# Moving attention transposes of two batches from TensorE to crossbar DMA, with the attention units on fixed slots

## The chip, the cores and the metric

One core of one Trainium2 chip. The metric is the device time of one execution in microseconds. Of every kernel there is one profiled execution and several timed ones, taken in turn with the kernel before on the same chip.

## The reference, cut to what matters

Four batches, 8 heads, 768 positions, head dimension 64. Each query attends to the keys within 16 positions and to 24 block summaries: the maximum of each block of 32 keys, with the mean of the block's values. The result, as 3072 tokens of 512 features, goes through a gated feed-forward layer.

```python
k_sum = k.reshape(B, H, nb, block, D).max(axis=3)
v_sum = v.reshape(B, H, nb, block, D).mean(axis=3)
scores_l = scale * np.matmul(q, k.transpose(0, 1, 3, 2))       # masked to |i - j| < 16
scores_s = scale * np.einsum('bhsd,bhnd->bhsn', q, k_sum) + np.log(block)
a = softmax(concatenate([scores_l, scores_s]))
x = (a @ concatenate([v, v_sum]))                              # 3072 x 512
out = (1 / (1 + np.exp(-(x @ w_gate))) * (x @ w_val)) @ w_out  # 512 -> 1536 -> 512
```

## The kernel before

The core works in four stages. Stage b runs the feed-forward of batch b on TensorE, and between its units ("m1": eight matmuls of 384 columns, "m2": six of 512) it places small units of the attention of batch b + 1. A stage has 24 m1 units and 12 m2 units, numbered 0 to 35 here as slots. The attention units:

```python
def T(self, p, h=None):            # a pair of heads: q and k to "dimension on partitions"
    ...                            # 12 TensorE transposes into PSUM (6 for k, 6 for q)
    self.natural(kTn[:, 16:16 + S], pk)                        # ScalarE copies PSUM -> SBUF
    self.natural(self.qT[p][:, 0:S if h is None else HALF], pq)
    nc.vector.tensor_reduce(out=kTx[:, 0, W:KX], ..., op=ALU.max)   # block maxima
    ...                            # two VectorE copies that spread keys and maxima
def S(self, p, hf): ...            # scores, exp on ScalarE, product with the mask on VectorE
def R(self, g, h): ...             # block sums of v, a quarter of four heads, VectorE
def M(self, g, h=None):            # means of four heads to bf16, four small DMAs to row group 96
    nc.vector.tensor_scalar_mul(out=mb, in0=self.ms[g], scalar1=1.0 / 32.0)
    for i in range(4):
        nc.sync.dma_start(out=self.vx[96:120, 0, 4 * g + i, 0:64], in_=mb[NS * i:NS * (i + 1)])
def B(self, *_): self.replicate(1) # ONE DMA, 272 KB: spreads the means over all 12 query tiles
def A(self, p, h=None): ...        # probabilities x [values; means]; needs what B wrote
def X(self, p, h=None): ...        # 6 TensorE transposes of the output, ScalarE copy to xT
# ... (cut)
MEANS = "R0a R0b R0c R0d M0 R1a R1b R1c R1d M1 - B".split()
NEXT = "- - T0 T1 S0a S0b T2 S1a S1b T3 S2a S2b S3a S3b - - A0 A1 X0 A2 X1 A3 X2 X3".split()
    both = [x for pair in zip(MEANS, NEXT) for x in pair]
    extra = (att[b + 1].units(" ".join(both)) + [lambda: loads(b + 2)]
             + att[b + 1].units(" ".join(NEXT[len(MEANS):])))
    spread(m1[0] + m1[1] + ffn.units2(), extra, 0, 33)
```

`spread` deals the 37 entries evenly over 33 slots. That puts M1 at about slot 16, B at slot 20 and the first A at slot 26 (entry number times 33/37).

The softmax here doesn't subtract the row's maximum and nothing guards it: scores larger than these inputs give would overflow.

## Time and profile before

| | before |
|---|---|
| median of 4 runs (range) | 262.46 us (262.02 to 262.8) |
| span of the profiled run | 259.5 us |
| until stage 1 starts / stage 1 / stage 2 / stage 3 | 95.2 / 57.2 / 56.5 / 46.8 us |
| TensorE idle in stage 1 / stage 2 | 0.8 / 0.0 us |

The prediction below shows the lines. How to read them: a row of a table by stretches gives the bounds in the span, the length, then per engine the busy time and the count of instructions. A row of a timeline gives start, length, engine, source line, operation, output<-inputs, shapes and count, and in brackets the idle time of the engine ahead of it and what ended that. A row of the list of waits gives who waited for what: total us, times, longest us. The row "PEclk" of a page is the clock that TensorE was granted, in tenths of full speed. TensorE's rows overlap at their ends, so a cost is read from one start to the next.

### The profile page before, as it was taken

What the parts mean: (1) busy time and instruction counts of PE and PEld (TensorE: products, weight loads), DVE (VectorE), ACT (ScalarE), POOL (GpSimd) and SP (SyncE); (2) the same over time, 40 slices, a digit from 0 to 9 for tenths busy, and PEclk for the clock granted to TensorE, in tenths of its full rate; (3) what the DMA queues carried; (4) which work ended last, traced back from release to release, by engine and by line L of the source; (5) the groups of instructions that cost most, each with busy time, mean ns of one, the idle gap of its engine ahead of it and who ended that gap; (6) DMA issues with size and microseconds to landing.
All of it is one profiled execution on the core that took longest, in us unless ns stands there. A gap on an engine that the chain in (4) does not pass through costs nothing.

```text
span 259.5 us, 5305 instructions
## 1 busy us (share of the span) xinstructions
PE 241.0 (93%) x2136; PEld 137.7 (53%) x2136; DVE 133.8 (52%) x263; ACT 124.5 (48%) x217; POOL 77.1 (30%) x111
## 2 busy tenths in 40 slices
PE   1567899999999998999999999999999999999993
PEld 1432455666644555666555556666555556666441
DVE  5865237648733318888645227988543124444000
ACT  2850347538942434766742435766533433333111
POOL 8998059377000279400002893000000000000000
PEclk9999999999999999999999999999999999999999
DMA  6999999999308999900199999000211220000132
GB/s 223 230 165 170 222 269 278 269 121 123 18 16 230 314 401 134 101 4 1 26 234 317 360 132 133 1 3 1 46 40 51 75 82 0 0 3 1 40 121 81
DMA packets 60912, 32.70 MB, mean 126 GB/s; under 512 B 40624, under 2 KB 57432, under 8 KB 60504
## 3 DMA queue, kind: packets, MB, share of 16 engines
q0 software_dynamic: 45632, 9.31, 41.4%
q1 hardware_dynamic: 14168, 22.28, 27.3%
q10 hardware_dynamic: 1088, 0.79, 0.9%
q8 instruction: 16, 0.26, 0.4%
q14 instruction: 8, 0.07, 0.1%
HBM read 34.34 MB, written 6.29 MB: 157 GB/s over the span
## 4 chain that ended last, share of the span: by engine, by line
PE 82%; DMA 9%; ACT 3%; DVE 2%; issue 1%; SPq 0%; ACTq 0%
PE gp L350 25%; PE vp L350 24%; PE m L367 19%; PE tp L178 4%; DMA qkst<-in_k_dram 3%; DMA out_dram<-ot 3%; PE sc L223 3%; PE vsp L240 3%; DMA qkst<-in_q_dram 3%; PE av L300 2%; PE br L321 2%; ACT kTn L184 1%; DVE kTx L199 1%; DVE vx L120 1%; ACT ot L372 1%
## 5 line engine op out<-in xcount | busy, mean ns | idle before, releaser
L358 DVE SCALAR_TENSOR_TENSOR hT<-gate,vp 128x384 bf16<-128x384 f32 x96 | 52.4, 548 | 56.1 <-PE vp L350 45.2
L350 PE MATMUL gp<-xT,wg 128*128 128x384 bf16 x384 | 80.2, 330 | 1.1 <-ACT xT L324 1.1
L350 PE MATMUL vp<-xT,wv 128*128 128x384 bf16 x384 | 79.6, 329 | 0.8 <-ACT ot L372 0.8
L367 PE MATMUL m<-wo,hT 128*128 128x512 bf16 x288 | 67.1, 380 | 0.0
L357 ACT ACTIVATE gate<-gp 128x384 f32<-128x384 f32 x96 | 47.4, 495 | 40.8 <-DVE hT L358 29.2
L350 PEld LDWEIGHTS <-wv 128*128 128x128 bf16 x384 | 37.8, 98 | 27.3 <-issue 3.0
L350 PEld LDWEIGHTS <-wg 128*128 128x128 bf16 x384 | 35.5, 99 | 21.7 <-issue 0.5
L122 POOL CAST qkbf<-qkst 128x768 bf16<-128x768 f32 (+1 forms) x28 | 22.5, 813 | 78.3 <-DMA qkst<-in_k_dram 38.6
L367 PEld LDWEIGHTS <-hT 128*128 128x128 bf16 x288 | 26.3, 98 | 28.4 <-issue 0.4
L372 ACT ACTIVATE ot<-m 128x512 f32<-128x512 f32 x24 | 14.3, 597 | 47.4 <-PE m L367 44.8
L147 POOL DMA_DIRECT2D vx<-in_v_dram x48 | 36.5, 774 | 0.6 <-DMA vx<-in_v_dram 0.4
L229 ACT ACTIVATE P<-sc 128x768 bf16<-128x768 f32 x32 | 26.0, 815 | 10.9 <-PE sc L223 10.8
L230 DVE TENSOR_TENSOR P<-P,mask 128x768 bf16<-128x768 bf16 x32 | 18.7, 585 | 13.3 <-ACT P L229 13.1
L178 PE MATMUL tp<-ident,qkbf 128*128 128x128 bf16 x192 | 15.5, 236 | 7.7 <-DVE qkbf L120 5.9
L199 DVE TENSOR_REDUCE kTx<-kTn 128x24 bf16<-128x768 bf16 x16 | 15.2, 951 | 7.8 <-ACT kTn L184 7.8
L178 PEld LDWEIGHTS <-qkbf 128*128 128x128 bf16 x192 | 13.4, 106 | 9.8 <-DVE qkbf L120 7.0
L324 ACT COPY xT<-br 128x768 bf16<-128x768 bf16 (+1 forms) x20 | 13.3, 669 | 10.9 <-PE br L321 10.9
L184 ACT COPY kTn<-tp 128x768 bf16<-128x768 bf16 x16 | 12.8, 799 | 9.3 <-PE tp L178 8.7
L268 DVE TENSOR_REDUCE ms<-vm 96x16 f32<-96x512 f32 x16 | 16.4, 1023 | 0.0
L309 DVE TENSOR_TENSOR xs<-av,rec 128x768 bf16<-128x768 f32 (+1 forms) x20 | 15.9, 797 | 0.7
L307 DVE RECIPROCAL rec<-av 128x12 f32<-128x12 f32 (+1 forms) x20 | 4.3, 216 | 22.3 <-PE av L300 22.3
L223 PE MATMUL sc<-qT,kTx 64*128 64x64 bf16 x384 | 12.1, 197 | 3.1 <-DVE kTx L203 2.9
(46 smaller groups left out, 112.0 us busy)
## 6 DMA issues: line engine op xcount, KB each, us to landing
qkst<-in_k_dram SPq DMA_DIRECT2D x16, 384.0 KB
out_dram<-ot SPq DMA_DIRECT2D x24, 256.0 KB
qkst<-in_q_dram SPq DMA_DIRECT2D x12, 384.0 KB
vx<-in_v_dram POOLq DMA_DIRECT2D x40, 96.0 KB, 4.7
vm<-in_v_dram SPq DMA_DIRECT2D x4, 768.0 KB
wo<-in_moe_w_out_dram POOLq DMA_DIRECT2D x6, 256.0 KB, 13.6
wg<-in_moe_w_gate_dram POOLq DMA_DIRECT2D x5, 256.0 KB, 8.0
wv<-in_moe_w_val_dram POOLq DMA_DIRECT2D x5, 256.0 KB, 9.8
```

The source lines that it names most:

```text
L122: nc.gpsimd.tensor_copy(out=out, in_=in_)
L147: nc.gpsimd.dma_start(out=vx_t[b % 2][r0:r0 + hi - lo, t, :, 0:64], in_=v[b, :, lo:hi, :].transpose([1, 0, 2]))
L178: nc.tensor.transpose(dst[:, 128 * t:128 * (t + 1)], src[:, t].rearrange("p h d -> p (h d)"), ident)
L199: nc.vector.tensor_reduce(out=kTx[:, 0, W:KX], in_=kTn[:, 16:16 + S].rearrange("p (n w) -> p n w", w=32), axis=AX.X, op=ALU.max)
L223: nc.tensor.matmul(out=sc[:, i, QT * t6:QT * (t6 + 1)], lhsT=kTx[64 * i:64 * i + 64, t, :], rhs=qT[64 * i:64 * i + 64, QT * t:QT * (t + 1) ...
L229: nc.scalar.activation(out=Ph, in_=sc[:, :, 0:6 * QT], func=ACT.Exp, scale=SCALE)
L230: nc.vector.tensor_tensor(out=Ph, in0=Ph, in1=mask[:, None, 6 * hf:6 * hf + 6, :].rearrange("p i t w -> p i (t w)") .to_broadcast([128, 2, ...
L350: nc.tensor.matmul(out=o, lhsT=wb[:, c, 128 * f:128 * (f + 1)], rhs=self.xT[:, c, HALF * hf:HALF * (hf + 1)], start=(c == 0), stop=(c == N ...
L357: nc.scalar.activation(out=gate, in_=gp, func=ACT.Tanh, scale=0.5)
L358: nc.vector.scalar_tensor_tensor(out=self.hT[hf][:, f, :], in0=gate, scalar=1.0, in1=vp, op0=ALU.add, op1=ALU.mult)
L367: nc.tensor.matmul(out=self.m3, lhsT=self.hT[hf][:, f, 128 * tt:128 * (tt + 1)], rhs=wo_bf[:, f], start=(f == 0), stop=(f == NF - 1))
L372: nc.scalar.mul(out=ot, in_=self.m3, mul=0.5)
```

## The change

The intent: TensorE is full, so 144 of its 288 transposes are given to DMA. q and k of batches 2 and 3 are loaded by casting DMAs of GpSimd in their natural layout ("nat") and transposed by DMAs of SyncE (D); the DMA writes what ScalarE copied before; the block maxima become a unit of their own (K). The attention output of these batches goes to xT by DMA (Y). The units are no longer dealt evenly but stand on slots.

```diff
+    def load_nat(tap, b):
+        nat = small()
+        for h in range(H):
+            nc.gpsimd.dma_start(out=nat[:, h // 2, :, 64 * (h % 2):64 * (h % 2) + 64],
+                                in_=tap[b, h].rearrange("(c p) d -> p c d", p=128))
+        return nat
...
+        def D(self, p, h=None):
+            self.begin(p)
+            for dst, nat in ((self.kTn[p][:, 16:16 + S], self.src[0]), (self.qT[p], self.src[1])):
+                nc.sync.dma_start_transpose(out=dst.rearrange("p (c t) -> p c t", c=6),
+                                            in_=nat[:, p].rearrange("p c d -> p (c d)"))
...
+        def Y(self, p, h=None):
+            c0, c1 = (0, 6) if h is None else (3 * h, 3 * h + 3)
+            nc.sync.dma_start_transpose(out=self.xT[:, p, ...], in_=self.xs[p][:, 0:c1 - c0]...)
...
-    MEANS = "R0a R0b R0c R0d M0 R1a R1b R1c R1d M1 - B".split()
-    NEXT = "- - T0 T1 S0a S0b T2 S1a S1b T3 S2a S2b S3a S3b - - A0 A1 X0 A2 X1 A3 X2 X3".split()
+    LATER = """
+        0 D0   1 D1 R0a   2 R0b   3 K0   4 R0c   5 D2   6 S0a R0d   7 K1 M0   8 S0b
+        9 D3 R1a   10 S1a   11 K2 R1b   12 S1b   13 R1c   14 S2a   15 K3 R1d   16 S2b M1
+        18 S3a B   20 S3b   22 A0   23 Y0   25 A1   26 Y1   27 A2   28 Y2   29 A3   30 Y3"""
+    def means(b):               # the two 768 KB loads of v for the block sums
+        if b < B:
+            att[b].L(0)
+            att[b].L(1)
...
+                at[0].append(lambda: loads(b + 2))
...
+                at[17].append(lambda: means(b + 2))
```

The buffers are rearranged too (staging in tiles of "nat" and "vm", four output tiles in place of two).

More of the change, by code (lines that the diff above doesn't have):

```diff
@@ L43 @@
     const = ctx.enter_context(tc.tile_pool(name="const", bufs=1))
-    stg_pool = ctx.enter_context(tc.tile_pool(name="stg", bufs=8))
     bf_pool = ctx.enter_context(tc.tile_pool(name="bf", bufs=10))
+    nat_pool = ctx.enter_context(tc.tile_pool(name="nat", bufs=4))
     vm_pool = ctx.enter_context(tc.tile_pool(name="vmp", bufs=2))
@@ L48 @@
     p_pool = ctx.enter_context(tc.tile_pool(name="pp", bufs=4))
-    xs_pool = ctx.enter_context(tc.tile_pool(name="xsp", bufs=2))
+    xs_pool = ctx.enter_context(tc.tile_pool(name="xsp", bufs=4))
     xT_pool = ctx.enter_context(tc.tile_pool(name="xTp", bufs=2))
@@ L122, in copy, with big, small, load_qk @@
             nc.gpsimd.tensor_copy(out=out, in_=in_)
-    def load_qk(tap, b, p, half=None, queue=None):
+    def big():
+        return vm_pool.tile([128, 2048], FP32, name="vm", tag="vm")
+    def small():
+        return nat_pool.tile([128, NP, 6, 128], BF16, name="nat", tag="nat")
+    def load_qk(tap, b, p, st, half=None, queue=None):
         n = S if half is None else HALF
@@ L128, in load_qk, with staging @@
         T = n // 128
-        st = stg_pool.tile([128, 2, 6, 64], FP32, name="qkst", tag="stg")
         (queue or nc.sync).dma_start(
-            out=st[:, :, 0:T, :].rearrange("p h t d -> p h (t d)"),
+            out=st.rearrange("p h t d -> p h (t d)"),
             in_=tap[b, 2 * p:2 * p + 2, s0:s0 + n, :].rearrange("h (p t) d -> p h (t d)", t=T),
         )
-        return st[:, :, 0:T, :]
+        return st
+    def staging(T):
+        raw = small().rearrange("p a c d -> p (a c d)").bitcast(FP32)
+        return [view(raw, 128 * T * i, [[64 * T, 2], [64, T], [1, 64]]) for i in range(12 // T)]
     def cast_qk(st, eng):
@@ L140, in cast_qk @@
         return bf
+    def load_nat(tap, b):
+        nat = small()
+        for h in range(H):
+            nc.gpsimd.dma_start(
+                out=nat[:, h // 2, :, 64 * (h % 2):64 * (h % 2) + 64],
+                in_=tap[b, h].rearrange("(c p) d -> p c d", p=128))
+        return nat
     def load_v(b, t0, t1):
@@ L172, in __init__ @@
             self.vx = vx_t[b % 2]
-            self.kTx, self.qT, self.P, self.xs = {}, {}, {}, {}
+            self.kTn, self.kTx, self.qT, self.P, self.xs = {}, {}, {}, {}, {}
             self.vm, self.ms = {}, {}
@@ L185, in natural, with begin @@
                            in_=src[:, 0:128 * T].rearrange("p (t a) -> p a t", t=T))
+        def begin(self, p):
+            self.kTn[p], self.kTx[p] = kTn_t[kT_ctr[0] % 2], kTx_t[kT_ctr[0] % 4]
+            kT_ctr[0] += 1
+            self.qT[p] = qT_pool.tile([128, S], BF16, name="qT", tag="qT")
+        def D(self, p, h=None):
+            self.begin(p)
+            for dst, nat in ((self.kTn[p][:, 16:16 + S], self.src[0]), (self.qT[p], self.src[1])):
+                nc.sync.dma_start_transpose(
+                    out=dst.rearrange("p (c t) -> p c t", c=6),
+                    in_=nat[:, p].rearrange("p c d -> p (c d)"))
         def T(self, p, h=None):
+            self.begin(p)
             at = psum2.tile([128, 2, 1024], BF16, name="tp", tag="at")
@@ L192, in T, with K @@
             self.transposed(pq, self.src[p][1])
-            kTn, kTx = kTn_t[kT_ctr[0] % 2], kTx_t[kT_ctr[0] % 4]
-            kT_ctr[0] += 1
-            self.kTx[p] = kTx
-            self.qT[p] = qT_pool.tile([128, S], BF16, name="qT", tag="qT")
-            self.natural(kTn[:, 16:16 + S], pk)
+            self.natural(self.kTn[p][:, 16:16 + S], pk)
             self.natural(self.qT[p][:, 0:S if h is None else HALF], pq)
+            self.K(p)
+        def K(self, p, h=None):
+            kTn, kTx = self.kTn[p], self.kTx[p]
             nc.vector.tensor_reduce(
@@ L260, in L @@
         def L(self, g, h=None):
-            st = self.vm[g] = vm_pool.tile([4 * NS, 32, 64], FP32, name="vm", tag="vm")
+            st = self.vm[g] = big()[0:4 * NS].rearrange("p (w d) -> p w d", d=64)
             nc.sync.dma_start(
@@ L314, in A @@
             self.xs[p] = xs
+        def Y(self, p, h=None):
+            c0, c1 = (0, 6) if h is None else (3 * h, 3 * h + 3)
+            nc.sync.dma_start_transpose(
+                out=self.xT[:, p, 128 * c0:128 * c1].rearrange("p (c t) -> p c t", c=c1 - c0),
+                in_=self.xs[p][:, 0:c1 - c0].rearrange("p c i d -> p (c i d)"))
         def X(self, p, h=None):
@@ L400 @@
     a0 = att[0]
-    sk = [load_qk(k, 0, p) for p in range(NP)]
-    sq = [load_qk(q, 0, p, half=0, queue=nc.scalar) for p in range(NP)]
+    raw = [big(), big()]
+    sk = [load_qk(k, 0, p, view(raw[p // 2], 768 * (p % 2), [[384, 2], [64, 6], [1, 64]]))
+          for p in range(NP)]
+    sq = [load_qk(q, 0, p, st, half=0, queue=nc.scalar) for p, st in enumerate(staging(3))]
     def cast0(p):
@@ L434 @@
     f0.m1(0, 0, 3, 4)
-    def load_next(b):
-        for p in range(NP):
-            s_ = (load_qk(k, b, p), load_qk(q, b, p))
-            srcs[b][p] = [cast_qk(s_[0], "pool"), cast_qk(s_[1], "pool")]
-    for p in range(NP):
-        srcs[0][p].append(cast_qk(load_qk(q, 0, p, half=1), "pool"))
+    for p, st in enumerate(staging(3)):
+        srcs[0][p].append(cast_qk(load_qk(q, 0, p, st, half=1), "pool"))
     for i in range(6):
         load_wo(i)
-    load_next(1)
+    for p in range(NP):
+        st = staging(6)
+        s_ = (load_qk(k, 1, p, st[0]), load_qk(q, 1, p, st[1]))
+        srcs[1][p] = [cast_qk(s_[0], "pool"), cast_qk(s_[1], "pool")]
     load_v(1, 0, NQ)
@@ L451 @@
     LAST = "- - A0 A1 X0 A2 X1 A3 X2 X3"
-    MEANS = "R0a R0b R0c R0d M0 R1a R1b R1c R1d M1 - B".split()
-    NEXT = "- - T0 T1 S0a S0b T2 S1a S1b T3 S2a S2b S3a S3b - - A0 A1 X0 A2 X1 A3 X2 X3".split()
-    def loads(b):
+    LATER = """
[3 more added lines that the diff above has]
+    def means(b):
         if b < B:
@@ L458, in loads @@
             att[b].L(1)
-            load_next(b)
+    def loads(b):
+        if b < B:
+            srcs[b][0], srcs[b][1] = load_nat(k, b), load_nat(q, b)
             load_v(b, 0, NQ)
@@ L466 @@
             spread(m1[0][1:], a0.units(REST), 2, 10)
-            extra = att[1].units(FIRST) + [lambda: loads(2)] + att[1].units(LAST)
+            extra = (att[1].units(FIRST) + [lambda: loads(2), lambda: means(2)]
+                     + att[1].units(LAST))
             spread(m1[1] + ffn.units2(), extra, 4, 23)
         else:
-            extra = []
+            base = m1[0] + m1[1] + ffn.units2()
+            at = {i: [] for i in range(len(base))}
             if b + 1 < B:
-                both = [x for pair in zip(MEANS, NEXT) for x in pair]
-                extra = (att[b + 1].units(" ".join(both)) + [lambda: loads(b + 2)]
-                         + att[b + 1].units(" ".join(NEXT[len(MEANS):])))
-            spread(m1[0] + m1[1] + ffn.units2(), extra, 0, 33)
+                at[0].append(lambda: loads(b + 2))
+                for w in LATER.split():
+                    if w.isdigit():
+                        slot = int(w)
+                    else:
+                        at[slot] += att[b + 1].units(w)
+                at[17].append(lambda: means(b + 2))
+            for i, u in enumerate(base):
+                u()
+                for x in at[i]:
+                    x()
 _INS = ['q', 'k', 'v', 'moe_w_gate', 'moe_w_val', 'moe_w_out']
```

## The prediction

> **What bounds the kernel now.** I read the page's busy line and the 40 slices first, to see whether one engine is full and from when.
>
> ```profile
> PE 241.0 (93%) x2136; PEld 137.7 (53%) x2136; DVE 133.8 (52%) x263; ACT 124.5 (48%) x217; POOL 77.1 (30%) x111
> ...
> PE   1567899999999998999999999999999999999993
> ...
> DMA  6999999999308999900199999000211220000132
> ...
> PE 82%; DMA 9%; ACT 3%; DVE 2%; issue 1%; SPq 0%; ACTq 0%
> ```
>
> TensorE is busy 93% of the span, and nearly all that is missing lies in the first slices, where inputs arrive. The chain that ended last is 82% TensorE too. "Busy" alone would not prove a bound, since matmuls are pipelined, so I next cut the span where the TensorE timeline starts the feed-forward of a new batch (31.91 to 32.11, 95.16, 152.40 and 208.85 us) and asked for the table by stretches. Its columns after the bounds are the length, then the busy time and count of TensorE, its weight loads, VectorE, ScalarE and GpSimd, then granted clock, DMA share, GB/s.
>
> ```profile
> 0.00:32.11 32.11, 18.66 (x165) 10.86 (x166) 18.55 (x51) 13.47 (x25) 23.54 (x42) 1.00 1.48 202
> 32.11:95.16 63.05, 62.69 (x654) 35.99 (x651) 33.28 (x64) 35.48 (x62) 26.71 (x36) 1.00 0.99 197
> 95.16:152.40 57.24, 56.46 (x530) 32.54 (x529) 34.30 (x62) 29.68 (x50) 21.52 (x28) 1.00 0.79 153
> 152.40:208.85 56.45, 56.45 (x530) 32.65 (x529) 34.41 (x62) 29.90 (x50) 5.30 (x8) 1.00 0.39 56
> 208.85:255.60 46.75, 46.75 (x265) 25.63 (x262) 13.30 (x24) 15.34 (x30) 0.00 (x0) 1.00 0.09 34
> ```
>
> The last stretch is pure feed-forward: 24 first-layer units and 12 second-layer half units, 36 units in 46.75 us, so 1.30 us each, at full clock and without a gap. The two before it hold the same feed-forward plus the attention of batch 2 and of batch 3; they are longer by 57.24 - 46.75 = 10.5 us and 56.45 - 46.75 = 9.7 us. TensorE has no idle time in them except one wait of 0.8 us. So each microsecond of TensorE work taken out of them comes off the end time, as long as nothing else comes to stop TensorE. VectorE (34 of 57 us), ScalarE (30) and the DMA engines have room.
>
> What one unit of attention costs is read from the timeline of TensorE as start to next start, not from the mean durations (236 ns per transpose there is a latency, and overlaps its neighbours):
>
> ```profile
> 158.25 0.81 PE L350 MATMUL vp<-xT,wv 128*128 128x384 bf16 x4
> 158.90 0.83 PE L178 MATMUL tp<-ident,qkbf 128*128 128x128 bf16 x12
> 159.57 0.81 PE L350 MATMUL gp<-xT,wg 128*128 128x384 bf16 x4
> ```
>
> ```profile
> 91.90 0.50 PE L321 MATMUL br<-ident,xs 128*128 128x128 bf16 x6
> 92.23 1.46 PE L367 MATMUL m<-wo,hT 128*128 128x512 bf16 x6
> ```
>
> Twelve transposes of one head pair (q and k) move the next matmul by 159.57 - 158.90 = 0.67 us, 56 ns each. The six that turn the attention output cost 92.23 - 91.90 = 0.33 us.
>
> **What the Trainium skill says.** (1) "TensorE: Matmul & The Clock Gate", Part 1, gives 55 to 56 ns from one warm 128-column matmul to the next; this trace agrees (56 ns). Its Part 4 gives about 275 ns for a transpose in a kernel's context; the trace shows a similar duration (236 ns) but not as a cost in the stream, and the stream is what counts here. (2) "VectorE: DVE Perf Modes", The three transpose paths, gives 1309 ns for a 128x128 bf16 block by crossbar DMA. (3) "DMA: Bandwidth & Descriptors", Latency and other measured facts, gives 261 GB/s as an effective rate of transposing DMA, and its section on the anatomy of a DMA about 2 us of fixed cost. (4) The same page, Issuing engines are not separate DMA queues: transfers of all issuers share the 16 DMA engines. The kernel before has no transposing DMA, so it neither confirms nor denies (2) and (3).
>
> **The change part by part.**
>
> Removed from TensorE: for batches 2 and 3, two times 4 head pairs with 12 + 6 transposes. That is 8 x 0.67 + 8 x 0.33 = 5.4 + 2.6 = 8.0 us. The PSUM space that they used is free as well. All of it lies in the two full stretches, thus on the path: **-8.0 us**.
>
> Removed from ScalarE: for each pair two copies of 0.80 us and one of 0.80 us, 8 x 2.4 = 19 us; from GpSimd sixteen casts of 0.86 us, 14 us. Both lie beside TensorE: no direct gain.
>
> Removed from the queue of SyncE: sixteen loads of 384 KB ahead of the output stores. At the start of batch 1 the stores of batch 0 stood behind such loads, ScalarE waited for an output buffer, and TensorE for ScalarE:
>
> ```profile
> 97.40 0.60 ACT L372 ACTIVATE ot<-m 128x512 f32<-128x512 f32 x1 [2.54 <-DMA out_dram<-ot]
> 98.05 0.81 PE L350 MATMUL vp<-xT,wv 128*128 128x384 bf16 x4 [0.78 <-ACT ot L372]
> ```
>
> Without those loads in that queue (only two loads of v, 768 KB each, stay) this wait should go: **-0.8 us**.
>
> Added to GpSimd's queue: 16 casting loads per batch. Twelve loads of v of the same kind (96 x 8 runs of 64 elements; the new ones have 128 x 6, also 768 runs) ran from about 55 to 66 us in the trace:
>
> ```profile
> 54.00:56.00 2.00, 1.00 0.33 51
> 56.00:58.00 2.00, 1.00 1.49 95
> ...
> 64.00:66.00 2.00, 1.00 1.77 108
> 66.00:68.00 2.00, 1.00 0.12 7
> ```
>
> So one takes about 0.95 us, and 16 take 15 us. The instruction order of the changed kernel has them right behind v of batch 1 with no wait for TensorE: k and q of batch 2 should land from 66 to 81 us, v of batch 2 until 93, k and q of batch 3 until 108, v of batch 3 until 120. Batch 2 is needed from 95 us on, so it is in time. It is hidden, but the traffic for batch 3 lies beside the first transposes by DMA.
>
> Added to SyncE's queue: 24 transposes of 128x768 bf16 (196,608 bytes). By (3), an estimate: 0.75 us of transfer + 2 us fixed = 2.8 us each. How much is allowed? The first pair's k is issued after the last store of batch 0, about 0.8 us into stage 1 (as store and next batch overlap before). Its consumer, the block maximum on VectorE, stands behind the fourth unit's gate product, 4 x 1.3 + 0.5 = 5.7 us into the stage: 5 us are allowed. After that VectorE is blocked and TensorE stops about two units later, as PSUM holds two open units; but the 1.7 us of VectorE work behind the wait (0.95 + 0.47 + 0.26) uses most of this. q is needed by the scores behind the seventh unit, 9.1 us into the stage: 8.3 us for two. The outputs' last transpose stands behind unit 30 of 36: 6 x 1.3 - 1.5 (division and store ahead of it) = 6.3 us until the next batch needs it. With 2.8 us each all of this fits. Beside the loads of batch 3 the rate may halve, which makes 3.6 us; still inside. I allow **+0.7 us** on average for stalls at the first pair of a stage and where new slots meet an engine's order.
>
> Moved: the attention units go to fixed slots, with the mask and sum work at the same rate; no count changes, 0 us. Start-up: buffers are shared otherwise, but each cast still waits for one load only, so 0 us.
>
> Sum: 262.6 - 8.0 - 0.8 + 0.7 = 254.5 us, 3.1% less.
>
> **The rivals.** First, **a slow transpose takes over**. If the six blocks of a transfer each cost the 1.3 us of (2), one transfer takes 7.9 us, the 12 of a stage 94 us against about 52 us of TensorE, and the kernel gets some 80 us slower. For it: nothing in the trace measures the operation. Against: 1.3 us for a lone block is mostly fixed cost if (3) holds, and the slots (two transfers per four units, 5.2 us) look placed for about 2.5 us each. Second, **a new wait in VectorE**: transposes of 5 to 7 us beside the loads of batch 3 stop VectorE at the first maximum, TensorE follows, and 1 to 3 us are lost in each stage: 256 to 260 us. For it: DMA share over 1.7 while such loads run. Against: only stage 1 has these loads. Third, **the transposes were hidden anyway**, in gaps of TensorE: time stays at 262. Against: TensorE shows no gaps in stages 1 and 2. Fourth, more is saved than counted: stage 1 is 10.5 us over pure feed-forward, of which 4 pairs at 1.0 us and the 0.8 us wait are known to go; if small restarts go too, 252 us.
>
> **Range and chances.** The saving of 8.0 us is counted and on the path, so the question is only what comes in its place. I take 251.5 to 258.5 as the range: all saved plus a little, or some 4 us lost again. 2% faster is below 257.3, which needs stalls under about 3.5 us in total: 0.78. Within 2%: 0.14. Slower by over 2% needs transposes near 6 us or more throughout: 0.08.
>
> **What would show it.** Right: the two stretches shrink from 57.2 and 56.5 to about 52.5 and 52.4 us, the start-up and last stretch stay within 0.5 us, TensorE transposes fall from 288 to 144, the wait for the output buffer near 97 us is gone, and transposing DMAs take 2.5 to 4 us from issue to landing. Wrong: VectorE's maximum waits for a DMA and TensorE then for VectorE; a first-layer unit at a stage's start waits for the turned output; or SyncE's queue is busy issuing through most of both stages.

## The result and the profile after

The changed kernel takes 270.47 us (median of 4 fast runs, 270.12 to 271.49) against 262.46 us. The ratio is 1.031 (95% interval 1.028 to 1.035). A ratio here is the mean time of one kernel's runs over that of the other's of the same rounds, so not quite the ratio of the medians. Executions over 1.5% slower than the fastest of the same kernel are left out of the means. The prediction, 254.5 us with 78% for faster, was wrong.

The busy line, the slices and the chain of the page after, to be held against those of before:

```profile
PE 236.3 (88%) x1979; PEld 131.3 (49%) x1992; DVE 135.5 (50%) x263; ACT 107.5 (40%) x193; POOL 90.2 (33%) x127
...
PE   1576898999999997899907999999969999999994
...
PEclk9997599999999999799995999999999999999999
...
PE 67%; DVE 10%; DMA 10%; issue 3%; ACT 2%; SPq 1%; ACTq 0%; DVEq 0%
```

TensorE does less work, but it now has holes: a slice of 0 near 138 us where it had been full, with a granted clock of about half (5) in the slice just behind it, and a clock of 0.7 near 110 us. The clock row does not show every slow stretch: in the kernel before it is full throughout, though the first group of stage 0 takes 1.28 us there (31.91 to 33.19 us). So slow groups are read below from one start to the next: four matmuls of 384 columns take 0.65 us at full speed. The chain that ended last has lost 15 points of TensorE and has a tenth of VectorE instead. The table by stretches (columns as in the prediction):

```profile
31.40:97.41 66.01, 63.56 (x649) 36.33 (x652) 35.45 (x64) 35.38 (x62) 47.05 (x62) 0.98 1.55 196
97.41:164.13 66.72, 55.95 (x454) 30.09 (x456) 34.52 (x62) 21.41 (x38) 18.97 (x24) 0.92 1.17 134
164.13:218.89 54.76, 52.36 (x454) 28.63 (x456) 33.73 (x62) 21.35 (x38) 0.00 (x0) 1.00 0.33 78
218.89:265.80 46.91, 46.80 (x263) 25.70 (x263) 13.29 (x24) 15.34 (x30) 0.00 (x0) 1.00 0.09 34
```

The count of TensorE instructions in stages 1 and 2 fell from 530 to 454 each (72 transposes gone, the rest are records missing from the trace). Yet stage 1 got 9.5 us longer, stage 2 only 1.7 us shorter, and stage 0, which the change hardly touches, 3.0 us longer. The list of what TensorE waited for names the places:

```profile
PE av L334 <- DMA vx<-vx: 10.0, 2, 7.8
...
PE vp L391 <- DVE hT L399: 2.4, 1, 2.4
```

`vx<-vx` is B, the DMA that spreads the means. TensorE's timeline there, and SyncE's queue just before:

```profile
135.05 0.25 PE L334 MATMUL av<-vx,P 120*64 120x65 bf16 x2
143.10 0.87 PE L334 MATMUL av<-vx,P 120*64 120x65 bf16 x22 [7.80 <-DMA vx<-vx]
143.90 1.46 PE L391 MATMUL gp<-xT,wg 128*128 128x384 bf16 x4
145.16 1.49 PE L391 MATMUL vp<-xT,wv 128*128 128x384 bf16 x4
146.44 0.64 PE L408 MATMUL m<-wo,hT 128*128 128x512 bf16 x1
```

```profile
130.83 1.47 SPq L311 DMA_DIRECT2D vx<-mb  x2
132.35 0.97 SPq L296 DMA_DIRECT2D vm<-in_v_dram  x2
133.51 0.86 SPq L319 DMA_DIRECT2D vx<-vx  x1
```

The two loads `vm<-in_v_dram` (1.5 MB) are issued just ahead of the copy. In the kernel before they stood behind it:

```profile
127.28 0.82 SPq L285 DMA_DIRECT2D vx<-vx  x1
128.15 2.26 SPq L262 DMA_DIRECT2D vm<-in_v_dram  x2
```

There the first group that needs the copy started at 135.76 us, 8.5 us after its issue, and did not wait. In the changed kernel TensorE stands ready at 135.30 us, 1.8 us after the issue. The chain of waits gives that copy 9.55 us in stage 1 and 4.25 us in stage 2, where there is no such load any more; even there TensorE waited 2.2 us. After the 7.8 us wait the next two groups of four matmuls take 1.26 and 1.28 us from start to start, in place of 0.65.

The other hole starts with a transposing DMA. On SyncE's queue, then on VectorE:

```profile
98.79 1.34 SPq L215 DMA_TRANSPOSE kTn<-nat  x1
```

```profile
106.44 0.95 DVE L233 TENSOR_REDUCE kTx<-kTn 128x24 bf16<-128x768 bf16 x1 [2.81 <-DMA kTn<-nat]
```

From the start of its issue to the block maximum that waited for it, the first transpose took 7.65 us, not 2.8. VectorE stood still, and TensorE lost 2.39 us plus 0.36 us for q, and then 1.44 us because three groups (110.01 to 113.40 us) again ran slower than 0.65 us.

### The profile page after: what moved, and what is told of

Same layout as the page of the kernel before. It is cut to its first block, busy times and chain, and to the rows that moved or that the text cites. A ratio compares the mean times of both kernels' runs of the same rounds, so it can differ in the third digit from the quotient of the medians.

```text
span 269.7 us, 5025 instructions
## 1 busy us (share of the span) xinstructions
PE 236.3 (88%) x1979; PEld 131.3 (49%) x1992; DVE 135.5 (50%) x263; ACT 107.5 (40%) x193; POOL 90.2 (33%) x127
## 3 DMA queue, kind: packets, MB, share of 16 engines
q0 software_dynamic: 70720, 12.46, 59.8%
## 4 chain that ended last, share of the span: by engine, by line
PE 67%; DVE 10%; DMA 10%; issue 3%; ACT 2%; SPq 1%; ACTq 0%; DVEq 0%
PE m L408 23%; PE gp L391 17%; PE vp L391 16%; DMA vx<-vx 5%; DMA qT<-nat 3%; PE av L334 3%; PE vsp L274 3%; DVE hT L399 3%; PE sc L257 2%; DVE kTx L233 2%; DVE P L264 2%; PE br L362 1%; DMA vx<-mb 1%; SPq L311 1%; DVE ms L302 1%
## 5 line engine op out<-in xcount | busy, mean ns | idle before, releaser
L391 PE MATMUL vp<-xT,wv 128*128 128x384 bf16 x384 | 81.5, 335 | 2.4 <-DVE hT L399 2.4
L391 PE MATMUL gp<-xT,wg 128*128 128x384 bf16 x384 | 82.1, 337 | 1.1 <-ACT xT L365 1.1
L399 DVE SCALAR_TENSOR_TENSOR hT<-gate,vp 128x384 bf16<-128x384 f32 x96 | 52.3, 548 | 59.3 <-PE vp L391 55.0
L408 PE MATMUL m<-wo,hT 128*128 128x512 bf16 x275 | 64.6, 381 | 0.9 <-issue 0.2
L408 PEld LDWEIGHTS <-hT 128*128 128x128 bf16 x288 | 27.2, 98 | 31.2 <-issue 1.2
L264 DVE TENSOR_TENSOR P<-P,mask 128x768 bf16<-128x768 bf16 x32 | 20.6, 647 | 11.5 <-ACT P L263 11.3
L334 PE MATMUL av<-vx,P 120*64 120x65 bf16 x384 | 11.2, 203 | 11.2 <-DMA vx<-vx 10.0
L334 PEld LDWEIGHTS <-P 120*64 120x64 bf16 x384 | 8.6, 116 | 18.3 <-DMA vx<-vx 10.3
L156 POOL DMA_DIRECT2D nat<-in_k_dram x16 | 13.3, 844 | 9.1 <-DMA vx<-in_v_dram 9.0
L197 PE MATMUL tp<-ident,qkbf 128*128 128x128 bf16 x96 | 8.9, 254 | 7.6 <-DVE qkbf L120 5.9
L257 PEld LDWEIGHTS <-kTx 64*128 64x128 bf16 x384 | 8.3, 98 | 13.3 <-issue 6.9
```

What stands on the lines that cost most here:

```text
L257: nc.tensor.matmul(out=sc[:, i, QT * t6:QT * (t6 + 1)], lhsT=kTx[64 * i:64 * i + 64, t, :], rhs=qT[64 * i:64 * i + 64, QT * t:QT * (t + 1) ...
L264: nc.vector.tensor_tensor(out=Ph, in0=Ph, in1=mask[:, None, 6 * hf:6 * hf + 6, :].rearrange("p i t w -> p i (t w)") .to_broadcast([128, 2, ...
L334: nc.tensor.matmul(out=av[r:r + 64, t // 6, (t % 6) // 2, i, 0:65], lhsT=P[0:KX, i, t, :], rhs=vx[0:KX, t, 2 * p + i, 0:65], start=True, s ...
L391: nc.tensor.matmul(out=o, lhsT=wb[:, c, 128 * f:128 * (f + 1)], rhs=self.xT[:, c, HALF * hf:HALF * (hf + 1)], start=(c == 0), stop=(c == N ...
L399: nc.vector.scalar_tensor_tensor(out=self.hT[hf][:, f, :], in0=gate, scalar=1.0, in1=vp, op0=ALU.add, op1=ALU.mult)
L408: nc.tensor.matmul(out=self.m3, lhsT=self.hT[hf][:, f, 128 * tt:128 * (tt + 1)], rhs=wo_bf[:, f], start=(f == 0), stop=(f == NF - 1))
```

## The experiments

Twelve kernels were run; the kernel before was run beside each. The theory after the first look: the saving is real, and late DMAs eat it, in three places. (1) The loads of v stand ahead of the copy B. (2) The first use of the means, A0, comes too soon after B. (3) The first transposes are issued too late for what they take beside other loads. Behind each long wait comes a stretch of slow clock. The rival: transposing DMAs as such slow the core down.

### The loads of v behind the copy

```diff
@@ -526,3 +526,3 @@
                         at[slot] += att[b + 1].units(w)
-                at[17].append(lambda: means(b + 2))
+                at[19].append(lambda: means(b + 2))
             for i, u in enumerate(base):
```

> The two 768 KB loads of v for the means of batch 3 move behind the copy that spreads the means of batch 2. Theory (the copy stands behind them on the queue): the copy takes 9.6 us in stage 1 and 4.3 us in stage 2 where no such load is ahead, so TensorE's wait for it in stage 1 falls from 7.8 to about 2.5 us, part of the slow clock after it goes, and the kernel takes about 264 us. Rival (the copy is slowed by GpSimd's loads of batch 3, or it simply starts too late): the wait stays at 6 us or more and the time stays at 269 to 270 us.

Measured: 263.47 us, ratio 1.004 (0.997 to 1.011). In SyncE's queue the order is now copy, then loads, and the chain of waits gives the copy half of its former time:

```profile
132.03 4.59 DMA vx<-vx
```

The loads now run beside the copy (issued at 132.91 us), and it is hardly slower than the 4.25 us without any, so standing behind them is what cost the time. TensorE's wait there fell from 7.80 to 4.35 us. The kernel got 7.2 us faster ((1.0313 - 1.0040) x 262.5), but only the 3.45 us of the wait are traced to the order of the DMAs. The profiled spans differ by 6.6 us (269.7 and 263.1): stage 1 is 5.4 us shorter (66.72 and 61.31), of which 3.45 us are the wait and about 1.4 us slow groups that did not follow the wait for the first pairs, and stage 1 starts 1.2 us sooner (96.2 and 97.4), ahead of the edit. So the expected 264 us came out in part by luck. The wait did not fall to 2.5 us as expected: the small copies ahead of it landed after 3.2 us in place of 1.8 us, and 4.35 us of lateness are left for place (2).

### No loads of GpSimd beside the first transposes (wrong result)

```diff
@@ -505,2 +505,5 @@
         if b < B:
+            if b == 3:
+                srcs[b][0], srcs[b][1] = srcs[2][0], srcs[2][1]
+                return
             srcs[b][0], srcs[b][1] = load_nat(k, b), load_nat(q, b)
```

> GpSimd's loads of q, k and v for batch 3 are left out; batch 3 computes with stale data, so its result is wrong on purpose. Theory (the transposes of the first pair are late because they share the DMA engines with these loads): VectorE's wait of 2.8 us and TensorE's of 2.4 us in stage 1 vanish with the slow clock behind them, 3.5 to 4.5 us in all, about 266 us; the wait of 7.8 us for the copy of the means stays, as these loads had ended before it. Rival (a transpose takes 7 us by itself): the waits stay.

Measured: 263.74 us (three fast runs), ratio 1.009 (1.002 to 1.017); the result is wrong (relative error 0.14). The profiled run was a slow one, so only its waits are used: TensorE's wait for VectorE's gate product and VectorE's for the first transpose are both gone:

```profile
98.03 1.32 SPq L215 DMA_TRANSPOSE kTn<-nat  x1
102.80 0.93 DVE L233 TENSOR_REDUCE kTx<-kTn 128x24 bf16<-128x768 bf16 x1
```

That transpose was issued at 98.03 us and its consumer ran at 102.80 us without waiting, so it took at most 4.8 us; beside GpSimd's loads it took 7.65 us. The wait for the copy of the means stayed (7.4 us), so these loads are not what slowed it. Both waits came out as the theory said; the time fell by 5.8 us by the ratios, more than the 3.5 to 4.5 us expected.

### The first two pairs transposed a stage earlier

```diff
@@ -494,3 +494,3 @@
     LATER = """
-        0 D0   1 D1 R0a   2 R0b   3 K0   4 R0c   5 D2   6 S0a R0d   7 K1 M0   8 S0b
+        0 -   1 R0a   2 R0b   3 K0   4 R0c   5 D2   6 S0a R0d   7 K1 M0   8 S0b
         9 D3 R1a   10 S1a   11 K2 R1b   12 S1b   13 R1c   14 S2a   15 K3 R1d   16 S2b M1
@@ -514,3 +514,3 @@
             extra = (att[1].units(FIRST) + [lambda: loads(2), lambda: means(2)]
-                     + att[1].units(LAST))
+                     + att[1].units(LAST) + att[2].units("D0 D1"))
             spread(m1[1] + ffn.units2(), extra, 4, 23)
@@ -527,2 +527,4 @@
                 at[17].append(lambda: means(b + 2))
+                if b + 2 < B:
+                    at[32] += att[b + 2].units("D0 D1")
             for i, u in enumerate(base):
```

> The transposes of the first two pairs of a batch are issued at the end of the stage before. Theory (they were issued too late for what they take): the wait in VectorE at the first block maximum goes, 3.5 to 4.5 us less, about 266 us, and the wait for the copy of the means stays at 7 to 8 us. Rival (the queue of SyncE is what is late): the same wait shows up at the third or fourth pair, time unchanged.

Measured: 266.12 us (three runs), ratio 1.018 (1.010 to 1.027), by the ratios some 3.4 us less than the changed kernel. No wait for a transpose is left in the list. TensorE arrives sooner at the first use of the means and waits longer there: 8.8 us in place of 7.8. So part of the gain is taken away by the next late DMA.

### The fixed slots with TensorE transposing

```diff
     def loads(b):
         if b < B:
-            srcs[b][0], srcs[b][1] = load_nat(k, b), load_nat(q, b)
+            for p in range(NP):
+                st = staging(6)
+                s_ = (load_qk(k, b, p, st[0]), load_qk(q, b, p, st[1]))
+                srcs[b][p] = [cast_qk(s_[0], "pool"), cast_qk(s_[1], "pool")]
             load_v(b, 0, NQ)
 # in LATER: D -> -, K -> T, Y -> X
```

> The fixed slots alone: q, k and the attention output are transposed by TensorE as before, on the slots of the change. Theory (the slots brought the end of the means too close to the first use): TensorE still waits some 7 us in stage 1 and 2 us in stage 2 for the copy of the means, and the kernel is slower than before, 268 to 276 us. Rival (the transposing DMAs themselves slow the copy and the rest): no such wait, and the time is that of before, 261 to 264 us.

Measured: 279.97 us, ratio 1.070 (1.065 to 1.075). This is slower than both kernels, and slower than expected. There is no transposing DMA in it, and TensorE's timeline shows the same wait:

```profile
143.12 0.87 PE L334 MATMUL av<-vx,P 120*64 120x65 bf16 x22 [7.75 <-DMA vx<-vx]
```

So the rival falls: the schedule alone makes that wait. What was not expected is another one of 2.54 us near 99 us, for ScalarE's output copy, with slow groups behind it; the kernel before has it with 0.78 us. Against this kernel with the same slots the transposing DMAs gain 9.5 us (279.97 - 270.47), or 10.1 us by the ratios, near the 8.8 us that the prediction counted. That is no clean measure, and the nearness is in part luck: this kernel loses 2.5 us, and 1.7 us more in slow groups, at the wait for the output copy, and the changed one loses as much at its first transposes (2.4 + 0.4 + 1.4 us).

### The wait filled with idle matmuls

```diff
@@ -527,2 +527,9 @@
                 at[17].append(lambda: means(b + 2))
+            def fill(n):
+                d = ps([128, 512], FP32, "fill")
+                for j in range(n):
+                    nc.tensor.matmul(out=d, lhsT=ident, rhs=wo_bf[:, j % NF], start=True, stop=True)
+
+            if b == 1:
+                at[22].insert(0, lambda: fill(32))
             for i, u in enumerate(base):
```

> The changed kernel with 32 idle matmuls of 512 columns (some 7 us of work with no use) put in front of the first use of the means in stage 1, where TensorE waited 7.8 us. Theory (a long wait makes the clock drop to half for about 3 us after it): the wait falls to about 1 us, the matmuls behind it run at 0.65 us a group and not at 1.3 us, and the kernel takes 1.5 to 2.5 us less, about 268.5 us, although TensorE does more work. Rival (the slow group comes from something else): the groups stay at 1.3 us and the time stays at 270 us or more.

Measured: 267.75 us (three runs), ratio 1.021 (1.014 to 1.028), by the ratios 2.7 us less than the changed kernel although TensorE does 7 us more of useless work. Its timeline:

```profile
131.25 7.07 PE L531 MATMUL fill<-wo,ident 128*128 128x512 bf16 x31
138.25 0.25 PE L334 MATMUL av<-vx,P 120*64 120x65 bf16 x2
139.52 0.57 PE L334 MATMUL av<-vx,P 120*64 120x65 bf16 x22 [1.02 <-DMA vx<-vx]
140.02 0.82 PE L391 MATMUL gp<-xT,wg 128*128 128x384 bf16 x4
140.68 0.81 PE L391 MATMUL vp<-xT,wv 128*128 128x384 bf16 x4
```

The groups behind the wait take 0.65 us again. So the slow groups come from TensorE's idling, and cost about 1.8 us behind one such wait (in the changed kernel's trace, against the same groups at full speed). In this profiled run the wait for the first transposes was shorter too (1.44 us, with no slow groups behind it); that is not the filling's doing. The Trainium skill names the cause in "TensorE: Matmul & The Clock Gate", Part 1: an idle window of about 3.4 us brings the array to half its clock. The traces agree for the long waits: each wait of 4.3 us and more in stages 0 to 2 was followed by groups at about half speed. For shorter waits they show more than the page says: of the waits of 2.1 to 2.6 us some were followed by slow groups too, as the 2.39 us of the changed kernel (with 0.36 us more just behind it) and the 2.54 us of the fixed slots with TensorE, and some were not, as the 2.60 us of the first experiment and the 2.2 us in stage 2 of the changed kernel.

### All three places repaired

```diff
@@ -494,5 +494,5 @@
     LATER = """
-        0 D0   1 D1 R0a   2 R0b   3 K0   4 R0c   5 D2   6 S0a R0d   7 K1 M0   8 S0b
+        0 -   1 R0a   2 R0b   3 K0   4 R0c   5 D2   6 S0a R0d   7 K1 M0   8 S0b
         9 D3 R1a   10 S1a   11 K2 R1b   12 S1b   13 R1c   14 S2a   15 K3 R1d   16 S2b M1
-        18 S3a B   20 S3b   22 A0   23 Y0   25 A1   26 Y1   27 A2   28 Y2   29 A3   30 Y3"""
+        18 S3a B   20 S3b   26 A0   27 Y0 A1   28 Y1 A2   29 Y2 A3   30 Y3"""
 
@@ -514,3 +514,3 @@
             extra = (att[1].units(FIRST) + [lambda: loads(2), lambda: means(2)]
-                     + att[1].units(LAST))
+                     + att[1].units(LAST) + att[2].units("D0 D1"))
             spread(m1[1] + ffn.units2(), extra, 4, 23)
@@ -526,3 +526,5 @@
                         at[slot] += att[b + 1].units(w)
-                at[17].append(lambda: means(b + 2))
+                at[19].append(lambda: means(b + 2))
+                if b + 2 < B:
+                    at[32] += att[b + 2].units("D0 D1")
             for i, u in enumerate(base):
```

> The transposing DMAs are kept, three places are repaired at once: loads of v behind the copy of the means, first two pairs transposed at the end of the stage before, and the use of the means (unit A) moved from slots 22 to 29 to slots 26 to 29. Theory (the removed TensorE work is a real saving of 8 us and the losses were late DMAs only): no wait of TensorE over 1 us in stages 1 and 2, each about 52.5 us long, 254 to 257 us in all. Rival (the transposing DMAs cost something else, spread out): stages stay above 54 us and the kernel takes 260 us or more.

Measured: 253.23 us, ratio 0.967 (0.963 to 0.971). The table by stretches:

```profile
95.87:148.50 52.63, 52.17 (x454) 28.52 (x456) 34.09 (x62) 21.38 (x38) 19.12 (x24) 1.00 1.55 171
148.50:200.78 52.28, 52.02 (x454) 28.53 (x456) 33.73 (x62) 21.38 (x38) 0.00 (x0) 1.00 0.30 80
```

The stages take 52.6 and 52.3 us; the prediction had named 52.5 and 52.4 us for a change that brings no new wait. The saving was there all the time.

The next three runs take one repair each away again, so that its worth beside the other two is seen.

### Repaired, but the loads of v ahead of the copy

```diff
@@ -526,3 +526,3 @@
                         at[slot] += att[b + 1].units(w)
-                at[19].append(lambda: means(b + 2))
+                at[17].append(lambda: means(b + 2))
                 if b + 2 < B:
```

> The repaired kernel without the first repair: the two loads of v stand ahead of the copy of the means again. The copy should take 9.5 us in place of 4.5 us. As the first use is four slots later than in the changed kernel, some of this is hidden: a wait of 3 to 5 us in stage 1 and up to 1.5 us of slow clock, 256 to 259 us. If the order of these loads does not matter once the use is later: 253 us.

Measured: 259.26 us, ratio 0.993 (0.988 to 0.997), 6.8 us lost by the ratios. In the profile the copy takes 7.65 us and TensorE waits 2.6 us; stage 1 is 57.4 us long, 4.8 us longer than in the repaired kernel. Group by group from one start to the next, 2.9 us of that lie at the wait (136.20 to 139.60 us for a group that takes 0.51 us in the repaired kernel), 1.5 us in the two slow groups behind it (139.60 to 142.99 us in place of 1.90 us), and 0.4 us in a short stall ahead of it, near 125.8 us. Stage 2 is as long as in the repaired kernel. The other 1.3 us of the spans' difference lie ahead of stage 1, where this edit changes nothing.

### Repaired, but the means used early

```diff
@@ -496,3 +496,3 @@
         9 D3 R1a   10 S1a   11 K2 R1b   12 S1b   13 R1c   14 S2a   15 K3 R1d   16 S2b M1
-        18 S3a B   20 S3b   26 A0   27 Y0 A1   28 Y1 A2   29 Y2 A3   30 Y3"""
+        18 S3a B   20 S3b   22 A0   23 Y0   25 A1   26 Y1   27 A2   28 Y2   29 A3   30 Y3"""
```

> The repaired kernel without the second repair: the means are used from slot 22 again. The chain of sums, small copies and the spreading copy ends about 5 us after that slot in stage 1 and 2 us in stage 2: waits of 4 to 6 and 2 us plus slow clock, 259 to 263 us. If the place of the use does not matter: 253 us.

Measured: 262.27 us, ratio 1.005 (1.000 to 1.009), 9.9 us lost: the largest of the three. TensorE waits 4.6 us in stage 1 and 2.3 us in stage 2 for the copy, although no load stands ahead of it; stage 1 is 59.8, stage 2 54.8 us long. So four slots between B and A0 are too few with the other two repairs in place as well.

### Repaired, but the first pairs transposed late

```diff
@@ -494,3 +494,3 @@
     LATER = """
-        0 -   1 R0a   2 R0b   3 K0   4 R0c   5 D2   6 S0a R0d   7 K1 M0   8 S0b
+        0 D0   1 D1 R0a   2 R0b   3 K0   4 R0c   5 D2   6 S0a R0d   7 K1 M0   8 S0b
         9 D3 R1a   10 S1a   11 K2 R1b   12 S1b   13 R1c   14 S2a   15 K3 R1d   16 S2b M1
@@ -514,3 +514,3 @@
             extra = (att[1].units(FIRST) + [lambda: loads(2), lambda: means(2)]
-                     + att[1].units(LAST) + att[2].units("D0 D1"))
+                     + att[1].units(LAST))
             spread(m1[1] + ffn.units2(), extra, 4, 23)
@@ -527,4 +527,2 @@
                 at[19].append(lambda: means(b + 2))
-                if b + 2 < B:
-                    at[32] += att[b + 2].units("D0 D1")
             for i, u in enumerate(base):
```

> The repaired kernel without the third repair: the first two pairs are transposed at slots 0 and 1 again. VectorE should wait some 3 us for them in stage 1 beside GpSimd's loads and TensorE 2.5 us, with slow clock behind it 3 to 4 us: 256 to 257 us. If the later use leaves room for this: 253 us.

Measured: 257.08 us (five runs), ratio 0.986 (0.980 to 0.992), 4.9 us lost by the ratios. In the profile TensorE waits 2.14 us behind VectorE for the first transpose (7.4 us from issue), and stage 1 is 2.0 us longer than in the repaired kernel; the slow clock that was expected behind the wait did not come. The profiled run also has a wait of 2.15 us for a weight load near 49 us, which no other profile shows; so the 4.9 us are more than this repair alone can account for, and about 2 us of them are.

By the ratios the three losses add to 21.6 us, more than the 16.9 us that lie between the changed and the repaired kernel ((1.0313 - 0.9668) x 262.5). Scatter ahead of stage 1 is part of these ratios. Counted in stages 1 and 2 of the profiles alone, the three losses are 4.8, 9.7 (7.2 + 2.5) and 2.0 us, together 16.5 us, against 16.6 us between the changed and the repaired kernel (14.1 + 2.5). So the three repairs account for the whole difference there. That they add up so closely need not hold in general: with the first pairs transposed earlier the next wait grew from 7.8 to 8.8 us.

### Repaired, the output turned by TensorE

```diff
-        18 S3a B   20 S3b   26 A0   27 Y0 A1   28 Y1 A2   29 Y2 A3   30 Y3"""
+        18 S3a B   20 S3b   26 A0   27 X0 A1   28 X1 A2   29 X2 A3   30 X3"""
```

> The repaired kernel with the attention output turned by TensorE again, q and k still by DMA. Theory (each transpose taken off TensorE is on the path): 8 x 0.33 = 2.6 us longer than the repaired kernel. Rival (TensorE has room by now, or these last transposes by DMA were themselves waited for): same time or shorter.

Measured: 256.65 us, ratio 0.979 (0.974 to 0.984): 3.3 us more than the repaired kernel by the ratios, against 2.6 us counted from the matmuls. Stages 1 and 2 are 54.5 and 54.0 us, 1.9 and 1.75 us longer, so each of the eight units costs 0.45 us where the stream of matmuls alone accounts for 0.33 us. TensorE's work really is on the path, transposes by DMA included.

### Stage 0: VectorE beside GpSimd

Stage 0 was 3 us longer in the changed kernel. Its timelines of VectorE and of GpSimd:

```profile
41.52 2.98 DVE L264 TENSOR_TENSOR P<-P,mask 128x768 bf16<-128x768 bf16 x1 [0.50 <-ACT P L263]
```

```profile
40.95 3.13 POOL L122 CAST qkbf<-nat 128x768 bf16<-128x768 f32 x4
```

A mask product that takes 0.56 us elsewhere took 2.98 us while GpSimd cast four tiles without a pause, and TensorE then waited 1.41 us for VectorE's next products. The Trainium skill has this in "SBUF — State Buffer", Who interferes with whom: a VectorE operation with both inputs in SBUF contends with GpSimd's reads, and the one that comes second is blocked. The trace agrees: the product started 0.57 us after the first cast and ended at 44.50 us, 0.4 us after the last. It was not new: in the kernel before the same product took 1.41 us beside three casts. The following two runs move the casts.

### Repaired, all values ahead of the casts

```diff
@@ -483,2 +483,3 @@
         load_wo(i)
+    load_v(1, 0, NQ)
     for p in range(NP):
@@ -487,3 +488,2 @@
         srcs[1][p] = [cast_qk(s_[0], "pool"), cast_qk(s_[1], "pool")]
-    load_v(1, 0, NQ)
```

> The repaired kernel with GpSimd issuing batch 1's loads of v before its casts of batch 1's q and k, not after. Theory (the stall of up to 2 us near 45 us is the mask product on VectorE, run beside four casts of GpSimd in a row): the mask product keeps 0.6 us there, stage 0 is about 63 us long, and the kernel takes 0.5 to 1.5 us less than the repaired one. Rival: the mask product is long for another reason, or the later casts hold up the transposes of batch 1: same time or longer.

Measured: 259.55 us, ratio 0.992 (0.987 to 0.996): a miss. The mask products did take 0.56 us, so that half of the theory held. But GpSimd's twelve loads of v waited for earlier DMAs, the casts came too late, and TensorE waited 4.3 us for them, until 62.2 us, with slow groups behind it. The rival as written down, too late a cast, came true.

### Repaired, two loads of values ahead of the casts

```diff
@@ -483,2 +483,3 @@
         load_wo(i)
+    load_v(1, 0, 2)
     for p in range(NP):
@@ -487,3 +488,3 @@
         srcs[1][p] = [cast_qk(s_[0], "pool"), cast_qk(s_[1], "pool")]
-    load_v(1, 0, NQ)
+    load_v(1, 2, NQ)
```

> The repaired kernel with only two of the twelve loads of v put ahead of GpSimd's casts of batch 1, so that the casts start some 5 us later, after the mask products near 42 us, but still well before the transposes at 58 us. Theory (mask products on VectorE are long only while GpSimd casts beside them): the products take 0.6 us, stage 0 gets up to 2.5 us shorter, and the kernel takes 1 to 2 us less than the repaired one. Rival: as before, the casts come too late, or the products stay long: same time or more.

Measured: 252.06 us, ratio 0.964 (0.959 to 0.969). The mask product and the casts are now apart:

```profile
40.88 0.56 DVE L264 TENSOR_TENSOR P<-P,mask 128x768 bf16<-128x768 bf16 x1 [0.51 <-ACT P L263]
```

```profile
46.50 5.56 POOL L122 CAST qkbf<-nat 128x768 bf16<-128x768 f32 x7
```

TensorE's wait of 2.6 us in stage 0 of the repaired kernel is gone; the longest one left there is 0.3 us, and in the profiles stage 0 is 2.1 us shorter (63.5 and 65.5 us). By the ratios the gain over the repaired kernel is 0.7 us, and the two intervals overlap, so it is likely but not certain. (The profiled run of the repaired kernel had begun stage 0 1.2 us sooner, with its first groups at full speed.) This version beats both kernels: 3.6% below the kernel before and 6.5% below the changed one (0.9641 / 1.0313).

| us in the profiled run | before | changed | repaired | casts later |
|---|---|---|---|---|
| until stage 1 | 95.2 | 97.4 | 95.9 | 95.0 |
| stage 1 | 57.2 | 66.7 | 52.6 | 52.3 |
| stage 2 | 56.5 | 54.8 | 52.3 | 52.3 |
| stage 3 | 46.8 | 46.9 | 46.9 | 46.9 |
| rest | 3.9 | 3.9 | 3.9 | 3.9 |
| span | 259.5 | 269.7 | 251.6 | 250.3 |

## Why the prediction was wrong

- **TensorE bounds stages 1 and 2, and removed transposes come off the end: right.** In the repaired kernel the two stages are within 0.2 us of the predicted 52.5 and 52.4 us, and giving the output transposes back to TensorE costs 3.3 us.
- **The wait for an output buffer goes (-0.8 us): right.** It is in no list of waits of a kernel with transposing DMAs, and came back with 2.5 us when the loads went back to SyncE's queue (fixed slots with TensorE).
- **"Moved: the attention units go to fixed slots ...; no count changes, 0 us": the step that failed.** It counted work and not distances. The chain R, M, B, A was not looked at; before, it was hidden: B stood some six slots ahead of A0 and the loads of v behind it. The change left four slots and put 1.5 MB of loads ahead of B on the same queue, so that TensorE was ready 1.8 us after the copy's issue in place of 8.5 us. That cost waits of 7.8 and 2.2 us, and about 1.8 us of slow clock. The order of SyncE's instructions, which was at hand, showed both (loads of `vm` ahead of the copy, where before they stood behind).
- **"2.8 us each ... 3.6 us" for a transposing DMA, and "+0.7 us" for stalls: mis-sized.** The 2 us in it are stated in "DMA: Bandwidth & Descriptors", in the section on the anatomy of a DMA, for DMAs that GpSimd issues; these are issued by SyncE. The first transpose took 7.65 us beside GpSimd's loads and at most 4.8 us without. It cost 2.4 + 0.4 us of waits and 1.4 us of slow clock. The second rival, a new wait in VectorE with 1 to 3 us lost, described it; it was given too little weight, and its count of two stages was one too many, as it had itself said that only stage 1 has these loads.
- **The end of GpSimd's loads was mis-sized too**: 120 us was predicted; the last one was issued near 124.6 us, and the DMA engines went quiet at 129 us. The loads waited for earlier ones of their own queue.
- **Full clock was taken for granted.** No term of the sum had what follows a wait.
- **"Start-up ... 0 us": wrong for stage 0**, which got 3.0 us longer; 1.95 us of it is the mask product beside GpSimd's casts (the timelines of before and after part between 44 and 48 us). Another 0.8 us lies in the first groups near 31 us, which run at half speed for longer in some profiles than in others; that is scatter, as the repaired kernel, with the same program up to there, ran them at full speed. The rest I have not assigned.

In sum for the profiled run: -8.8 us as predicted; +7.8 and +2.2 (copy of the means), +2.8 (first transposes), +3.2 (slow clock behind both), +3.0 (stage 0), and -0.7 because the start-up ahead of stage 0 ended that much sooner; together +9.5 us, against a difference of the spans of 269.7 - 259.5 = 10.2 us. I have not assigned the other 0.7 us.

What stays open: how long a transposing DMA takes with no other traffic (only "at most 4.8 us" is shown), and how much of the differences by ratios lies in the scatter ahead of stage 1. The repaired slots with TensorE transposing everything were not run; that the full 8 us are saved there is read from the lengths of stages 1 and 2, and the run that gives back the output transposes tests a third of it.

## What to carry to other kernels

When units of work are put in another order, count for each DMA the time between its issue and its first use in the new order, and look at what stands ahead of it on the same queue; equal counts of instructions say nothing about that. When the bound engine idles for a few microseconds, add what its clock loses behind the wait. A change that measures slower can hold a full saving: compare its stages with the floor that the counted work gives, and look for the waits that lie between.

## What the Trainium skill lacked or had wrong

- "DMA: Bandwidth & Descriptors", Latency and other measured facts: the effective rate of 261 GB/s, with the 2 us of fixed cost that its section on the anatomy of a DMA states for GpSimd's path, gave an estimate of 2.8 us for a transpose of 128x768 bf16 from SBUF to SBUF. The runs show 7.65 us (7.4 us in another run) beside GpSimd's loads of runs of 64 elements, and at most 4.8 us without. The page gives no time for a transpose beside other traffic.
- The same page gives the time that a queue needs to issue a transpose only for "previous generations" in general, in cycles, and not for this chip and this size: here 1.21 us at least, and up to 3.1 us beside the loads, while an output store took 0.33 us.
- "TensorE: Matmul & The Clock Gate", Part 4: it says that full clock does not engage for transposes and gives about 275 ns for one. Here twelve of them in a stream of matmuls took 0.67 us, 56 ns each, which is the full-clock spacing of Part 1. Whether transposes with no matmuls among them would keep the clock up, no run here shows.
- The same page, Part 1, does not say what a single idle gap shorter than its window does: here a wait of 2.54 us was followed by four groups that took 4.3 us in place of 2.6 us, and one of 2.60 us by none.
